# Attention over pooled pixels, then a gated MLP: the second batch's pixels loaded uncast, added in rows by GpSimd and pooled in pairs, and 17 GELU chunks on VectorE

## The chip, the cores and the metric

The kernel runs on one core of one Trainium2 chip. The metric is the device time of one launch in microseconds; a kernel's time is the median over its runs. A profile is one execution with the hardware profiler on; its span goes from the first to the last instruction of the program.

## The reference

Four batches of 12,288 queries attend to keys made from 384 x 32 pixels of 128 channels. Pixels are averaged over 4 x 4 windows, which leaves 768 rows per batch, and one product with `w_sr` gives both keys and values. The result goes through a two-layer MLP with a sigmoid-gated GELU.

```
kv_pool = kv.reshape(B, H // 4, 4, W // 4, 4, C).mean(axis=(2, 4))
k = v = kv_pool.reshape(B, -1, C) @ w_sr            # 768 x 128 for each batch
a = softmax((q @ k.transpose(0, 2, 1)) / sqrt(C))
x = (a @ v).reshape(B * 12288, C)
h = x @ w_in                                        # d_ff = 2048
out = (h * (1 / (1 + exp(-1.702 * h)))) @ w_out
```

## The kernel before

The 49,152 queries are cut into 96 groups of 512 (`NG`), 24 to a batch. A batch's 768 keys are six chunks of 128 (`JC`), the 2,048 hidden units 16 chunks (`FCH`). The work has four stages: attention for groups 0 to 47, the MLP for them, attention for groups 48 to 95, the MLP for them. In the trace they begin at about 9, 145, 490 and 607 us.

A step is a pair of a TensorE part and one ScalarE instruction. `fill_attn` (L340, L342) makes the scores of up to three chunks in a set of three PSUM banks, and ScalarE takes their exponential into one of 102 slots of `ag`; `fill_moe` (L586, L588) does the same for the MLP with GELU. The drains use the slots up: `drain_attn` multiplies the exponentials with the values (L353, 129 columns, the last one giving the sum), and VectorE divides (L376, L379) into the resident tile `x`; `drain_moe` (L596) multiplies with `w_out`, VectorE transposes the result (L607) and SP's queue stores it. `x` holds 24,576 query rows. It is stored to HBM and loaded back transposed in parts (`put_away` L493, `bring_back` L499, both on SP's queue), since the MLP wants it with channels on partitions.

The order of every queue is written at build time by one loop at the end of the function. It keeps a running time `now`, counted in steps of about one 512-column matmul, predicts when ScalarE and VectorE finish (`end`, `dve`, with the costs `FIXED`, `CHUNK`, `COST`, `COPY`, `RECIPROCAL`), and places fills two steps ahead of ScalarE with drains and small extras between them. At run time each engine takes its instructions in that order and waits on semaphores. Four PSUM banks serve as accumulators for the drains and extras; after the narrow opening steps two of them remain.

Some chunks never go to ScalarE. `rolling` score chunks and the scores of groups 48 to 51 (`early`) are computed by TensorE in `early_fill` (L405) and exponentiated by VectorE with a polynomial (`early_exp`). `lent` chunks of the last stage are GELUs computed by VectorE (`lent_gelu`, L443 to L465, after the matmul L399); they go into `aside`, a ring of three chunks. A drain of a group with a lent chunk is placed only when the plan says that the chunk is made.

`background(i)` and `background_moe(g)` run when the first step of a group is placed. They put DMAs on the queues: `cast_q` (L209, GpSimd's queue) casts 2,048 queries from float32 to bfloat16 in HBM, at the groups in `CAST`; `load_qT` (L215, SP's queue) loads them transposed into one of four `qT` buffers, at the groups in `TURN`. `gate()` writes one number on VectorE and overwrites it on GpSimd, so that GpSimd's queue doesn't run ahead of VectorE's place in the order. The weights of the MLP are loaded at groups 27 and 28 (L541, L544).

Keys come about in two ways. Batches 2 and 3 are summed by accumulating DMAs (`add_kv`, L173) during the MLP stages. Batches 0 and 1 are pooled by TensorE: `load_chunk` (L130, GpSimd's queue) loads 128 half pixel rows, cast to bfloat16, into a part of `x` that is not yet used; `pool_chunk` (L139) multiplies them with the 0/1 matrix `sum4`, 16 matmuls of 32 columns that sum four pixel rows and four pixels of a row; VectorE copies the result (L142), and `key_and_value` (L161 to L164) makes the chunk of keys and of values. For batch 1 the six loads are put on the queue at groups 10 and 12, the pools become extras at groups 15 to 20 and the keys one group later each; group 24 is the first that needs them.

```
if i in (10, 12):
    gate()
    for jc in range(i % 10 * 3 // 2, i % 10 * 3 // 2 + 3):
        load_chunk(1, jc)
```

Of the kernel before, what the change touches and what calls it, by code (L numbers as in the profile page):

```python
# [7 lines left out]
F32 = mybir.dt.float32  # L8
F32R = mybir.dt.float32r
I32 = mybir.dt.int32  # L10
BF = mybir.dt.bfloat16
AF = mybir.ActivationFunctionType
AX = mybir.AxisListType
ADD = mybir.AluOpType.add
# [10 lines left out]
def kernel(  # L25
    ctx, tc, q, kv, w_sr, moe_w_in, moe_w_out, out,
):
    nc = tc.nc
    B, N, C = q.shape
    _, H, W, _ = kv.shape  # L30
    r = 4
    Hp, Wp = H // r, W // r
    J = Hp * Wp
    JC = J // 128
    d_ff = moe_w_in.shape[1]
    FCH = d_ff // 128
    scale = 1.0 / (C ** 0.5)
    G = 512
    SG = 4 * G
    NG = B * N // G  # L40
    NS = NG // 4
    GB = NG // B
# [10 lines left out]
    kv_r = kv.rearrange("b (ch p) (a w) c -> b a ch p (w c)", p=128, a=2)  # L53
# [6 lines left out]
    XS = NS // R  # L60
# [7 lines left out]
    kvtmp = ctx.enter_context(tc.tile_pool(name="kvtmp", bufs=1))  # L68
# [3 lines left out]
    opool = ctx.enter_context(tc.tile_pool(name="op", bufs=3))  # L72
# [12 lines left out]
    def acc(key=None):  # L85

        nonlocal last_acc
        last_acc = next_acc()
        turns.append(last_acc)
        turns.remove(last_acc)  # L90
        if key:
            closes[last_acc] = key
        return banks[:, last_acc, :]

    def next_acc():
        return min((m for m in turns if m not in closes), key=lambda m: (max(free[m], now), turns.index(m)))
# [12 lines left out]
    x = xpool.tile([128, XS * SG], BF, name="x")  # L109

    def x_tile(s):
        return x[:, s % XS * SG:(s % XS + 1) * SG]
# [3 lines left out]
    HC = H // 128  # L116
    h = J // 2
    kv_tiles, kv_sums, pooled, pTs, kTs, vs = {}, {}, {}, {}, {}, {}

    def new_keys(b):  # L120
        kTs[b] = kvres.tile([128, J], BF, name="kT")

        vs[b] = kvres.tile([128, JC, C + 8], BF, name="v")
        nc.vector.memset(vs[b][:, :, C:C + 1], 1.0)

    def load_chunk(b, jc):

        a, ch = divmod(jc, HC)
        t = x_tile(XS - 1 - jc)
        nc.gpsimd.dma_start(out=t, in_=kv_r[b, a, ch])  # L130
        kv_tiles[b, jc] = t.rearrange("p (wp w1 c) -> p w1 wp c", w1=r, c=C)

    def pool_chunk(b, jc):
# [7 lines left out]
        pTs[b, jc] = kvtmp.tile([128, 128], BF, name="pTc", bufs=2)  # L141
        nc.vector.tensor_copy(pTs[b, jc], ps[:, 0:128])  # L142

    def key_chunk(b, jc):
        if jc == 0:
            new_keys(b)
        ps = acc()
        nc.tensor.matmul(ps[:, 0:128], w_sr_sb, pTs[b, jc], start=True, stop=True)
        nc.vector.tensor_copy(kTs[b][:, jc * 128:jc * 128 + 128], ps[:, 0:128])
# [5 lines left out]
        vs[b, jc] = True  # L155

    def key_and_value(b, jc):
        if (b, jc) == (1, 0):
            new_keys(b)
        ps = acc()  # L160
        nc.tensor.matmul(ps[:, 0:128], w_sr_sb, pTs[b, jc], start=True, stop=True)  # L161
        nc.tensor.matmul(ps[:, 128:256], pTs.pop((b, jc)), w_sr_sb, start=True, stop=True)
        nc.vector.tensor_copy(kTs[b][:, jc * 128:jc * 128 + 128], ps[:, 0:128])  # L163
        nc.vector.tensor_copy(vs[b][:, jc, 0:C], ps[:, 128:256])  # L164
        vs[b, jc] = True
# [41 lines left out]
    def cast_q(s):  # L207
        sl = slice(s * SG, (s + 1) * SG)
        nc.gpsimd.dma_start(out=q_bf[sl, :].rearrange("(p i) c -> p (i c)", p=128),  # L209
                            in_=q_flat[sl, :].rearrange("(p i) c -> p (i c)", p=128))  # L210

    def load_qT(s):
        qTs[s] = qpool.tile([128, 1, SG], BF, name="qT")
        nc.vector.memset(qTs[s][:, 0, 0:1], 0.0)
        nc.sync.dma_start_transpose(out=qTs[s], in_=q_bf[s * SG:(s + 1) * SG, :])  # L215
# [53 lines left out]
    for m in range(0, 128, 32):  # L269
        p = slice(m, m + 32)  # L270
# [3 lines left out]
    sum4 = cpool.tile([128, 32], BF)  # L274
# [3 lines left out]
    w_sr_sb = cpool.tile([128, C], BF)  # L278
# [40 lines left out]

    early = range(NG // R, NG // R + EARLY)  # L320
    rolling = [(i, JC - 1) for i in [*range(38, NG // R, 6), *range(57, 90, 6)]]
    lent = [(g, FCH - 1) for g in range(52, 94, 3)]
    aside = agpool.tile([128, K, 512], BF, name="aside")

    def weights(c):
# [112 lines left out]
    def lent_gelu(ps, out):  # L438
# [23 lines left out]
        for m in (0, 256):  # L462
            nc.vector.reciprocal(b[:, m:m + 256], a[:, m:m + 256])  # L463
            yield RECIPROCAL
        nc.vector.scalar_tensor_tensor(out, raw, -LN2 / 1.702, b, MUL, MUL)  # L465
# [21 lines left out]
    PART, FIRST = 24, 3  # L487

    def put_away(n, m):
        size = PART // 2 if n == 0 and m > FIRST else PART  # L490
        for o in range(m * PART, m * PART + PART, size):
            lo = n * XS * SG + o * T
            nc.sync.dma_start(out=x_bf[lo:lo + size * T, :].rearrange("(k p) c -> p k c", p=T),  # L493
                              in_=x[:, o * T:(o + size) * T].rearrange("p (k c) -> p k c", k=size))

    def bring_back(n, m):
        o = m * PART
        lo = n * XS * SG + o * T
        nc.sync.dma_start_transpose(out=x[:, o * T:(o + PART) * T].unsqueeze(1), in_=x_bf[lo:lo + PART * T, :])  # L499
# [6 lines left out]
    def gate():  # L506

        one = gate_tile[:, gates[0] % 8:gates[0] % 8 + 1]
        gates[0] += 1
        nc.vector.memset(one, 0.0)  # L510
        nc.gpsimd.memset(one, 0.0)  # L511

    TURN = {6: 3, 7: 4, 8: 5, 20: 6, 21: 7, 22: 8, 30: 9, 32: 10, 35: 11, 40: 12}
    CAST = {0: [5], 13: [6], 14: [7], 15: [8], 25: [9, 10], 26: [11, 12]}
    CAST_MOE = {20: 13, 21: 14, 22: 15, 23: 16, 33: 17, 34: 18, 35: 19, 36: 20, 37: 21, 38: 22, 39: 23}

    def background(i):

        first_round = i < GB * 2
        s = TURN.get(i, NS) if first_round else i // 4 + 3 if i % 4 == 0 else NS  # L520
        if s < NS:
            load_qT(s)
        if i in CAST:
            gate()
            for s in CAST[i]:
                cast_q(s)
        if i in (10, 12):
            gate()
            for jc in range(i % 10 * 3 // 2, i % 10 * 3 // 2 + 3):
                load_chunk(1, jc)  # L530
        if 0 <= i - 16 < JC:
            extras.append((key_and_value, 1, i - 16))
        if 0 <= i - 15 < JC:
            extras.append((pool_chunk, 1, i - 15))
        if i in (28, 33, 38):
            put_away(0, (i - 28) // 5)
        if i in (31, 36, 41):
            bring_back(0, (i - 31) // 5)
        if i == 27:
            gate()  # L540
            nc.gpsimd.dma_start(out=w_in_sb, in_=moe_w_in)  # L541
        if i == 28:
            gate()
            nc.gpsimd.dma_start(out=w_out_sb, in_=moe_w_out.rearrange("(o p) c -> p o c", p=128))  # L544

# [33 lines left out]
    extras = []  # L579
# [67 lines left out]
    for n in range(R):  # L647
        part = [c for c in chunks if c[0] // (NG // R) == n]
        while part:
            m = sizes.pop(0) if sizes else K  # L650
# [12 lines left out]
        while flat:  # L663
            m = K if len(flat) > sum(rest) else rest.pop(0)
# [25 lines left out]
    def jobs(p):  # L690

        nonlocal now
        for f, *args in first.get(p, ()):
            if f in COST:
                now = max(now, free[next_acc()])
            f(*args)
            if f in COST:
                now += COST[f][0]
                free[last_acc] = copied(f)

    def prepare(p):

        nonlocal now
        kind, part = seq[p]
        for i, jc in part:
            if (kind, i) not in begun:
                begun.add((kind, i))
                (background if kind == "a" else background_moe)(i)
            while kind == "a" and ((key_and_value, i // GB, jc) in extras or (transpose_q, i) in extras):
                f, *args = extras.pop(0)  # L710
                now = max(now, free[next_acc()]) + COST[f][0]
                f(*args)
                free[last_acc] = copied(f)
# [20 lines left out]


    FIXED, CHUNK, SWITCH, HANDOVER, EVACUATE = 0.295, 1.978, 6.0, 1.0, 4.5
    COST = {pool_chunk: (1.9, 2.6), key_chunk: (0.3, 2.4), value_chunk: (0.3, 2.4),
            transpose_q: (1.05, 4.2), early_fill: (1.0, 5.5), key_and_value: (0.55, 3.5),
            transpose_pooled: (0.9, 3.6), make_k: (0.8, 3.2), make_v: (0.8, 3.7)}
    COPY = {pool_chunk: 1.5, key_chunk: 1.5, value_chunk: 1.5, key_and_value: 2.8, transpose_q: 3.2}  # L740
    SMALL = 0.26
    RECIPROCAL = 10.5
    PAUSE = 4.0
    end, extra_at = [], 0.0
    source, dve = None, 0.0
# [2 lines left out]
    def on_dve(cost):  # L748
        nonlocal dve
        dve = max(dve, now + 1.0) + cost  # L750


    def copied(f):
        if f not in COPY:
            return now + COST[f][1]
        on_dve(COPY[f])
        return max(now + COST[f][1], dve)

# [28 lines left out]
    for n in range(len(seq)):  # L787
        fill(n + 2)
        jobs(n + 3)
        while True:  # L790
# [33 lines left out]
            kind, i, c = source[0]  # L824
# [11 lines left out]
            start = now if source is todo_early else max(now, end[needs] + HANDOVER)  # L836
            if first_of:
                start = max(start, bank)
# [44 lines left out]
```

The softmax here doesn't subtract the row's maximum and nothing guards it: scores larger than these inputs give would overflow.

## Time and profile before

| | |
|---|---|
| time, median of 8 runs | 950.9 us (950.64 to 952.19) |
| profiled execution, its own time | 952.19 us |
| span of that execution | 950.4 us |
| ScalarE instructions, GELU over three chunks (L588) | 1,508 ns each as recorded, 510 with the narrower ones |
| TensorE matmuls of 512 columns (L586) | 379 ns each as recorded, x1522 |
| VectorE GELU, reciprocal of 256 columns (L463) | 1,726 ns, x28 |
| q loads, transposing (L215) | 4.4 us from issue to landing (median of 21) |
| pixel loads of batch 0 and 1 (L130) | 9.3 us from issue to landing (median of 12) |

The recorded lengths of matmuls and ScalarE instructions overlap, since the engines work in a pipeline; how often they start says more than how long one is. An engine's row of busy time counts neither its DMA issues nor its waits on semaphores. The first 13 us are the opening: loads of pixels and queries, the first pools and keys. After the last ScalarE instruction, at about 945 us, the last products, copies and stores follow.

### The profile page before, as it was taken

What the parts mean: (1) busy time and instruction counts of PE and PEld (TensorE: products, weight loads), DVE (VectorE), ACT (ScalarE), POOL (GpSimd) and SP (SyncE); (2) the same over time, 40 slices, a digit from 0 to 9 for tenths busy, and PEclk for the clock granted to TensorE, in tenths of its full rate; (3) what the DMA queues carried; (4) which work ended last, traced back from release to release, by engine and by line L of the source; (5) the groups of instructions that cost most, each with busy time, mean ns of one, the idle gap of its engine ahead of it and who ended that gap; (6) DMA issues with size and microseconds to landing.
All of it is one profiled execution on the core that took longest, in us unless ns stands there. A gap on an engine that the chain in (4) does not pass through costs nothing.

```text
span 950.4 us, 15424 instructions
## 1 busy us (share of the span) xinstructions
PE 940.6 (99%) x6314; PEld 502.8 (53%) x6314; DVE 536.6 (56%) x1037; ACT 933.9 (98%) x708; POOL 67.1 (7%) x115
## 2 busy tenths in 40 slices
PE   7999999999999999999999999999999999999998
PEld 4677677444444444444446777754444444444444
DVE  5643553102477777778655775465666665556631
ACT  5999999999999999999999999999999999999998
POOL 4101001330000242000000000000000000000000
DMA  9999931999876899764435683662222222222222
GB/s 181 208 176 188 206 69 35 156 125 171 166 136 100 125 149 126 116 107 78 67 56 105 133 163 80 134 122 34 44 34 45 34 46 34 45 33 45 34 45 45
DMA packets 372871, 94.93 MB, mean 100 GB/s; under 512 B 346736, under 2 KB 370416, under 8 KB 372464
## 3 DMA queue, kind: packets, MB, share of 16 engines
q1 hardware_dynamic: 343872, 61.31, 36.8%
q0 software_dynamic: 28656, 32.51, 22.6%
q8 instruction: 49, 0.80, 0.4%
q14 instruction: 22, 0.18, 0.1%
q10 hardware_dynamic: 272, 0.13, 0.0%
HBM read 52.49 MB, written 48.76 MB: 107 GB/s over the span
## 4 chain that ended last, share of the span: by engine, by line
ACT 88%; PE 9%; DMA 2%; issue 0%; DVE 0%; POOL 0%; POOLq 0%
ACT ag L588 71%; ACT ag L342 17%; PE banks L340 4%; PE banks L353 3%; DMA qT<-q_bf 1%; DMA x<-in_kv_dram 1%; PE banks L139 0%; PE banks L586 0%; PE banks L624 0%; ACT L588 0%; PE banks L596 0%; PE banks L233 0%; ACT L342 0%; DVE kT L163 0%; POOL x L222 0%
## 5 line engine op out<-in xcount | busy, mean ns | idle before, releaser
L588 ACT ACTIVATE ag<-banks 128x1536 bf16<-128x1536 f32 (+1 forms) x510 | 682.2, 1508 | 0.0
L586 PE MATMUL banks<-x,w_in_sb 128*128 128x512 bf16 x1522 | 411.7, 379 | 0.1
L596 PE MATMUL banks<-ag,w_out_sb 128*128 128x512 bf16 x1506 | 407.8, 379 | 0.0
L342 ACT ACTIVATE ag<-banks 128x1536 bf16<-128x1536 f32 (+2 forms) x192 | 245.8, 1442 | 5.0 <-PE banks L340 4.7
L596 PEld LDWEIGHTS <-w_out_sb 128*128 128x128 bf16 x1520 | 148.4, 98 | 178.1 <-issue 0.9
L586 PEld LDWEIGHTS <-w_in_sb 128*128 128x128 bf16 x1522 | 147.3, 98 | 170.4 <-issue 1.1
L607 DVE STREAM_TRANSPOSE o_sb<-banks 128x512 f32<-128x512 f32 x95 | 67.9, 715 | 210.9 <-PE banks L596 201.7
L353 PEld LDWEIGHTS <-ag 128*128 128x128 bf16 x2272 | 146.1, 98 | 46.4 <-issue 0.6
L353 PE MATMUL banks<-v,ag 128*128 128x129 bf16 x2272 | 163.7, 220 | 0.1
L340 PE MATMUL banks<-qT,kT 128*128 128x512 bf16 x544 | 148.7, 379 | 1.6 <-DVE kT L163 1.0
L432 DVE SCALAR_TENSOR_TENSOR ea<-ea,eb 128x512 f32<-128x512 f32 x128 | 87.9, 687 | 3.2
L376 DVE RECIPROCAL rec<-banks 128x3 f32<-128x3 f32 x124 | 22.2, 179 | 96.0 <-PE banks L353 96.0
L379 DVE TENSOR_TENSOR x<-banks,rec 128x384 bf16<-128x384 f32 x124 | 69.1, 558 | 4.3
L340 PEld LDWEIGHTS <-kT 128*128 128x128 bf16 x544 | 46.3, 98 | 26.6 <-DVE kT L163 1.7
L463 DVE RECIPROCAL eb<-ea 128x256 f32<-128x256 f32 x28 | 47.6, 1726 | 0.5
L173 POOL DMA_DIRECT2D kvs<-in_kv_dram x32 | 40.5, 1311 | 17.2 <-DMA kvs<-in_kv_dram 13.7
L421 DVE TENSOR_SCALAR ea<-banks 128x512 f32<-128x512 f32 x32 | 22.1, 691 | 34.0 <-PE banks L405 33.7
L456 DVE SCALAR_TENSOR_TENSOR ea<-ea,eb 128x512 f32<-128x512 f32 x56 | 38.3, 685 | 1.6
L511 POOL MEMSET gate_tile<- 1x1 f32 x37 | 3.9, 105 | 327.9 <-DVE gate_tile L510 327.9
L427 DVE SCALAR_TENSOR_TENSOR eb<-eb,ea 128x512 f32<-128x512 f32 x32 | 22.1, 690 | 0.9
L443 DVE TENSOR_SCALAR qT<-banks 128x512 f32<-128x512 f32 x14 | 9.7, 691 | 17.2 <-PE banks L399 16.9
L434 DVE SCALAR_TENSOR_TENSOR ag<-ea,ee 128x512 bf16<-128x512 f32 x24 | 16.5, 688 | 0.7
(84 smaller groups left out, 266.1 us busy)
## 6 DMA issues: line engine op xcount, KB each, us to landing
out_dram<-o_sb SPq DMA_DIRECT2D x380, 64.0 KB, 2.0
kvs<-in_kv_dram POOLq DMA_DIRECT2D x32, 384.0 KB, 6.4
q_bf<-in_q_dram POOLq DMA_DIRECT2D x21, 512.0 KB, 6.7
x_bf<-x SPq DMA_DIRECT2D x12, 768.0 KB, 5.7
x<-in_kv_dram POOLq DMA_DIRECT2D x12, 512.0 KB, 9.3
x_bf<-x SPq DMA_DIRECT2D x8, 384.0 KB, 4.6
x<-in_q_dram POOLq DMA_DIRECT2D x5, 256.0 KB, 15.1
w_in_sb<-in_moe_w_in_dram POOLq DMA_DIRECT2D x1, 512.0 KB, 11.6
```

The costliest lines, as they stand in the source:

```text
L173: nc.gpsimd.dma_start(out=kv_sums[b][:, i2], in_=kv_p[b, i, w, :, i2], **({"accum_op": ADD} if n else {}))
L340: nc.tensor.matmul(ps[:, k, :], kTs[i // GB][:, jc * 128:(jc + 1) * 128], rhs, start=True, stop=True)
L342: nc.scalar.activation(place([("a",) + c for c in chunks]), ps, AF.Exp, scale=scale)
L353: nc.tensor.matmul(av_of[u][:, k * (C + 1):(k + 1) * (C + 1)], weights(("a", i, jc))[:, o:o + T], vs[i // GB][:, jc, 0:C + 1], start=(jc = ...
L379: nc.vector.tensor_tensor(to, ps[:, :, 0:C], rec.unsqueeze(2).broadcast_to([128, TS, C]), MUL)
L432: nc.vector.scalar_tensor_tensor(a, a, COEFFS[k], b, ADD, MUL)
L456: nc.vector.scalar_tensor_tensor(a, a, COEFFS[k], b, ADD, MUL)
L463: nc.vector.reciprocal(b[:, m:m + 256], a[:, m:m + 256])
L586: nc.tensor.matmul(ps[:, k, :], w_in_sb[:, fc * 128:(fc + 1) * 128], x[:, g % (4 * XS) * G:(g % (4 * XS) + 1) * G], start=True, stop=True)
L588: nc.scalar.activation(place([("m",) + c for c in chunks]), ps, AF.Gelu_apprx_sigmoid)
L596: nc.tensor.matmul(o_of[g], w_out_sb[:, fc, :], weights(("m", g, fc)), start=(fc == 0), stop=(fc == FCH - 1))
L607: nc.vector.transpose(o_sb, o_of.pop(g))
```

## The change

Batch 1's pixels are loaded in float32, without a cast, from SP's queue (`load_pixels`), three chunks at group 10 and one each at groups 11, 12 and 13, into three places in `x` of twice the size; chunks 3 to 5 reuse the places of chunks 0 to 2. GpSimd adds the four pixels of a row for each pooled column with three tensor additions per chunk (`sum_pixels`, groups 11 to 16), the last of them into bfloat16, in a buffer of the output pool. TensorE then sums over the four pixel rows alone, two chunks at a time (`pool_sums`, 8 matmuls of 32 columns, extras at groups 16, 19 and 22), and `key_pair` makes two chunks of keys and values at groups 17, 20 and 23. The planner gets costs for the two.

The lent GELU chunks of the last stage are those of 17 groups instead of 14, and the planner's cost of a VectorE reciprocal is lower. The cast of q tile 9 goes from group 25 to 16, its load from group 30 to 24; tiles 10 to 12 are cast in two and one instead of with tile 9; the weights of the MLP are loaded one group earlier each. Parts 2 and 3 of the first stage's `x` are stored in halves, as the later ones were.

```diff
--- before.py
+++ after.py
@@ -141,6 +141,51 @@
         pTs[b, jc] = kvtmp.tile([128, 128], BF, name="pTc", bufs=2)
         nc.vector.tensor_copy(pTs[b, jc], ps[:, 0:128])
 
+    held, sums = {}, {}
+
+    def load_pixels(jc):
+
+        a, ch = divmod(jc, HC)
+        o = (XS - JC) * SG + jc % 3 * 2 * SG
+        t = x[:, o:o + 2 * SG].bitcast(F32)
+        if jc < 3:
+            nc.vector.memset(t[:, 0:1], 0.0)
+        nc.sync.dma_start(out=t, in_=kv_r[1, a, ch])
+        kv_tiles[1, jc] = t.rearrange("p (wp w1 c) -> p w1 wp c", w1=r, c=C)
+
+    def sum_pixels(jc):
+
+        t = kv_tiles.pop((1, jc))
+        if jc % 2 == 0:
+            held[jc // 2] = opool.tile([128, 512], F32, name="o_sb").bitcast(BF)
+        sums[jc] = held[jc // 2][:, jc % 2 * 512:jc % 2 * 512 + 512].rearrange("p (wp c) -> p wp c", c=C)
+        nc.gpsimd.tensor_tensor(t[:, 0], t[:, 0], t[:, 1], ADD)
+        nc.gpsimd.tensor_tensor(t[:, 2], t[:, 2], t[:, 3], ADD)
+        nc.gpsimd.tensor_tensor(sums[jc], t[:, 0], t[:, 2], ADD)
+
+    def pool_sums(b, jc):
+
+        ps = acc()
+        for k in range(2):
+            for wp in range(4):
+                o = k * 128 + 32 * wp
+                nc.tensor.matmul(ps[:, o:o + 32], sums[jc + k][:, wp, :], sum4, start=True, stop=True)
+        pTs[b, jc] = kvtmp.tile([128, 256], BF, name="pTp")
+        nc.vector.tensor_copy(pTs[b, jc], ps[:, 0:256])
+
+    def key_pair(b, jc):
+        if jc == 0:
+            new_keys(b)
+        ps = acc()
+        pT = pTs.pop((b, jc))
+        nc.tensor.matmul(ps[:, 0:256], w_sr_sb, pT, start=True, stop=True)
+        for k in range(2):
+            nc.tensor.matmul(ps[:, 256 + k * 128:384 + k * 128], pT[:, k * 128:(k + 1) * 128], w_sr_sb,
+                             start=True, stop=True)
+        nc.vector.tensor_copy(kTs[b][:, jc * 128:(jc + 2) * 128], ps[:, 0:256])
+        nc.vector.tensor_copy(vs[b][:, jc:jc + 2, 0:C], ps[:, 256:512].rearrange("p (k c) -> p k c", k=2))
+        vs[b, jc] = vs[b, jc + 1] = True
+
     def key_chunk(b, jc):
         if jc == 0:
             new_keys(b)
@@ -155,8 +200,6 @@
         vs[b, jc] = True
 
     def key_and_value(b, jc):
-        if (b, jc) == (1, 0):
-            new_keys(b)
         ps = acc()
         nc.tensor.matmul(ps[:, 0:128], w_sr_sb, pTs[b, jc], start=True, stop=True)
         nc.tensor.matmul(ps[:, 128:256], pTs.pop((b, jc)), w_sr_sb, start=True, stop=True)
@@ -319,7 +362,7 @@
 
     early = range(NG // R, NG // R + EARLY)
     rolling = [(i, JC - 1) for i in [*range(38, NG // R, 6), *range(57, 90, 6)]]
-    lent = [(g, FCH - 1) for g in range(52, 94, 3)]
+    lent = [(g, FCH - 1) for g in range(52, 94) if g % 5 in (2, 4)]
     aside = agpool.tile([128, K, 512], BF, name="aside")
 
     def weights(c):
@@ -487,7 +530,7 @@
     PART, FIRST = 24, 3
 
     def put_away(n, m):
-        size = PART // 2 if n == 0 and m > FIRST else PART
+        size = PART // 2 if n == 0 and m > 1 else PART
         for o in range(m * PART, m * PART + PART, size):
             lo = n * XS * SG + o * T
             nc.sync.dma_start(out=x_bf[lo:lo + size * T, :].rearrange("(k p) c -> p k c", p=T),
@@ -510,8 +553,8 @@
         nc.vector.memset(one, 0.0)
         nc.gpsimd.memset(one, 0.0)
 
-    TURN = {6: 3, 7: 4, 8: 5, 20: 6, 21: 7, 22: 8, 30: 9, 32: 10, 35: 11, 40: 12}
-    CAST = {0: [5], 13: [6], 14: [7], 15: [8], 25: [9, 10], 26: [11, 12]}
+    TURN = {6: 3, 7: 4, 8: 5, 20: 6, 21: 7, 22: 8, 24: 9, 32: 10, 35: 11, 40: 12}
+    CAST = {0: [5], 13: [6], 14: [7], 15: [8], 16: [9], 25: [10, 11], 26: [12]}
     CAST_MOE = {20: 13, 21: 14, 22: 15, 23: 16, 33: 17, 34: 18, 35: 19, 36: 20, 37: 21, 38: 22, 39: 23}
 
     def background(i):
@@ -524,22 +567,25 @@
             gate()
             for s in CAST[i]:
                 cast_q(s)
-        if i in (10, 12):
-            gate()
-            for jc in range(i % 10 * 3 // 2, i % 10 * 3 // 2 + 3):
-                load_chunk(1, jc)
-        if 0 <= i - 16 < JC:
-            extras.append((key_and_value, 1, i - 16))
-        if 0 <= i - 15 < JC:
-            extras.append((pool_chunk, 1, i - 15))
+        if 10 <= i < 10 + JC:
+            if i > 10:
+                sum_pixels(i - 11)
+            for jc in range(3) if i == 10 else [i - 8] if i < 14 and i > 10 else []:
+                load_pixels(jc)
+        if i == 10 + JC:
+            sum_pixels(JC - 1)
+        if i in (16, 19, 22):
+            extras.append((pool_sums, 1, (i - 16) // 3 * 2))
+        if i in (17, 20, 23):
+            extras.append((key_pair, 1, (i - 17) // 3 * 2))
         if i in (28, 33, 38):
             put_away(0, (i - 28) // 5)
         if i in (31, 36, 41):
             bring_back(0, (i - 31) // 5)
-        if i == 27:
+        if i == 26:
             gate()
             nc.gpsimd.dma_start(out=w_in_sb, in_=moe_w_in)
-        if i == 28:
+        if i == 27:
             gate()
             nc.gpsimd.dma_start(out=w_out_sb, in_=moe_w_out.rearrange("(o p) c -> p o c", p=128))
 
@@ -706,7 +752,7 @@
             if (kind, i) not in begun:
                 begun.add((kind, i))
                 (background if kind == "a" else background_moe)(i)
-            while kind == "a" and ((key_and_value, i // GB, jc) in extras or (transpose_q, i) in extras):
+            while kind == "a" and ((key_pair, i // GB, jc // 2 * 2) in extras or (transpose_q, i) in extras):
                 f, *args = extras.pop(0)
                 now = max(now, free[next_acc()]) + COST[f][0]
                 f(*args)
@@ -734,12 +780,12 @@
 
 
     FIXED, CHUNK, SWITCH, HANDOVER, EVACUATE = 0.295, 1.978, 6.0, 1.0, 4.5
-    COST = {pool_chunk: (1.9, 2.6), key_chunk: (0.3, 2.4), value_chunk: (0.3, 2.4),
+    COST = {pool_chunk: (1.9, 2.6), pool_sums: (1.1, 3.2), key_pair: (1.1, 5.0), key_chunk: (0.3, 2.4), value_chunk: (0.3, 2.4),
             transpose_q: (1.05, 4.2), early_fill: (1.0, 5.5), key_and_value: (0.55, 3.5),
             transpose_pooled: (0.9, 3.6), make_k: (0.8, 3.2), make_v: (0.8, 3.7)}
-    COPY = {pool_chunk: 1.5, key_chunk: 1.5, value_chunk: 1.5, key_and_value: 2.8, transpose_q: 3.2}
+    COPY = {pool_chunk: 1.5, pool_sums: 2.1, key_pair: 4.2, key_chunk: 1.5, value_chunk: 1.5, key_and_value: 2.8, transpose_q: 3.2}
     SMALL = 0.26
-    RECIPROCAL = 10.5
+    RECIPROCAL = 8.2
     PAUSE = 4.0
     end, extra_at = [], 0.0
     source, dve = None, 0.0
```

## The prediction

> **What bounds the kernel now.** I read the page first: busy shares, then the windows of the last stage, then the chain of waits and the list of waits for the few places where the busy engines stop.
>
> ```profile
> PE 940.6 (99%) x6314; PEld 502.8 (53%) x6314; DVE 536.6 (56%) x1037; ACT 933.9 (98%) x708; POOL 67.1 (7%) x115
> ```
>
> Two engines are full at once, TensorE and ScalarE. A busy TensorE row is modelled, so it must be counted. Windows of 50 us in the last stage, TensorE's first, ScalarE's second:
>
> ```profile
> 650.00:700.00 50.00, 50.00 (x233) 1.00 0.25 39
> 700.00:750.00 50.00, 50.00 (x233) 1.00 0.27 42
> ```
> ```profile
> 650.00:700.00 50.00, 50.00 (x38) 1.00 0.25 39
> 700.00:750.00 50.00, 50.00 (x39) 1.00 0.27 42
> ```
>
> 233 matmuls of 512 columns in 50 us, with one cut at each edge, are one per 0.2165 us, the pace of three in 0.65 us that the chain shows elsewhere. So TensorE's queue really has no hole, and neither has ScalarE's. What either saves comes out of the time only as far as the other saves as much. The chain in order of time (start, length, what):
>
> ```profile
> 41.31 0.65 PE banks L340 x3
> 41.95 0.85 PE banks L353 x15
> ...
> 56.38 0.65 PE banks L340 x3
> 57.03 0.39 PE banks L139 x16
> ...
> 93.21 8.70 DMA qT<-q_bf
> 101.90 0.05 issue
> 101.95 0.39 PE banks L405
> ...
> 103.19 5.33 ACT ag L342 x4
> ...
> 620.89 29.52 ACT ag L588 x22
> ```
>
> It gives all prices: 0.0565 us for a value matmul (15 in 0.85), 0.0245 us for a pooling one (16 in 0.39), 1.342 us for one ScalarE instruction over three chunks (22 in 29.52). It also shows the one large hole after the first 20 us: at 93.21 a transposing load of q is issued, lands 8.7 us later, and L405, an early score matmul for VectorE, waits for it. In the list of waits of 100 to 144 us (total, times, longest):
>
> ```profile
> ACT ag L342 <- PE banks L340: 1.4, 1, 1.4
> PEld L405 <- DMA qT<-q_bf: 1.5, 1, 1.5
> ```
>
> TensorE stands still from 100.4 to 101.9 and ScalarE with it for 1.4 us; both then run on without a hole, so it is lost to the end. Windows of 6 us, the last two columns being the share of the DMA engines and GB/s:
>
> ```profile
> 42.00:48.00 6.00, 2.19 (x6) 1.00 1.07 211
> 48.00:54.00 6.00, 1.23 (x5) 1.00 1.06 211
> 54.00:60.00 6.00, 0.00 (x0) 1.00 1.25 262
> 60.00:66.00 6.00, 0.00 (x0) 1.00 0.43 91
> ```
>
> Six pixel loads and three casts of q, each reading 1 MB, fill the DMA engines from about 41.5 (where three q transposes end) to about 63: 2.4 us each.
>
> **What the Trainium skill says.** "Perfetto Trace Analysis", Identifying the Most-Contended Engine: matmul busy time is no measure of how close TensorE is to its limit. Agreed: I count pitches. "TensorE: Matmul & The Clock Gate", Back-to-back issue gap: N/2.4 + 2.5 ns, and about 25 ns as a floor; the trace has 216.5 ns at 512 columns and 24.5 ns at 32, so a 32-column matmul is all floor, and fewer of them is the only saving. "DMA: Bandwidth & Descriptors", Issuing engines are not separate DMA queues: they share 16 engines. So moving the loads from GpSimd's queue to SP's gives no bandwidth; no run here shows it yet. "SBUF — State Buffer", SBUF: two separate sides: GpSimd and VectorE lock each other out where VectorE reads two SBUF inputs or uses a two-port mode. Between 41 and 70 us VectorE runs L376, L379 and copies, all with their large input from PSUM, so I count no conflict; the trace has no GpSimd add to test it.
>
> **The change part by part.**
>
> *TensorE, pooling.* Out: 6 x 16 pooling matmuls, 96 x 0.0245 = 2.35 us. In: 24, 0.59 us. The key and value matmuls keep their columns (12 of 128 against 3 of 256 and 6 of 128): 0.67 us either way. Saved: 1.76 us.
>
> *ScalarE, 17 lent chunks in place of 14.* Three chunks fewer make 245 instead of 246 three-chunk instructions in the last stage: 1.34 us. TensorE computes the lent scores anyway, so nothing there.
>
> *VectorE for it.* One lent chunk from the group rows is 0.69 + 3 x 0.43 + 0.69 + 0.42 + 4 x 0.69 + 0.69 + 0.42 + 2 x 1.73 + 0.66 = 11.1 us; three more are 33 us, on an engine that is 56% busy. What matters is lateness. In the trace a lent chunk takes 12.6 to 15.2 us from first to last instruction and is then used 11.7 to 19.3 us later. Counting matmuls in the changed program's order, the use stands 24.3 us or more behind its score matmul, and starts are at least 15.1 us apart. 15.2 of 24.3 leaves 9 us. Cost: nothing; if the cover were gone, TensorE would wait.
>
> *The q load of tile 9*, with its cast, moves from group 30 to 24. A group lasts 2.68 us (two steps of 1.34), so 93.2 becomes about 77; with the same 8.7 us it lands by 86, and L405 wants it at 100.4. The 1.5 us hole goes: 1.4 us on ScalarE. Next late could be its cast, now behind the adds on GpSimd's queue: issued near 64.5, it has 12 us; casts took 6.0 to 13.3 us to land while three stood in line, so this is close but covered by 14 us more. On SP the first storing of x (74.97 before) now stands behind this load and starts by 82; its reload, held behind the q load until 98.2 before, follows from about 88. Neither is needed before the stage at 143.7. Weight loads one group earlier: nothing.
>
> *GpSimd's adds.* 18 additions of 512 elements. The trace has none. "GPSIMD Engine Reference", 3.1, has 4497 ns for 2048 elements; a quarter is 1.12 us, and I take 1.2 with dispatch (an estimate). Bounds: 0.77 us (its one-input rate at 512 elements) and 2.2 (twice the quarter, for strided rows and the type change). The first pixels land near 41.5 + 2.4 + 0.6 = 44.6, as SP issues them when its q transposes are out (39.5). Then 3.6 us a chunk, plus 0.55 for a gate and cast at the third to sixth: sums of chunks 1, 3 and 5 end at 51.8, 60.1 and 68.4. The loads of chunks 3 to 5 wait for the sum three before and land within some 4.5 us; each has two sums, 7 us, to do so. In the changed order the three pools stand 2.4, 10.3 and 18.2 us of matmuls behind the place where the first pool ran (53.1): 55.5, 63.4, 71.3. Spare: 3.7, 3.3, 2.9 us. So the adds cost nothing as long as one takes less than about 1.34 us (44.6 + 18t + 2.2 = 71.0). Behind a late add stand on GpSimd the casts of q 7 to 9, on SP the pixel loads and then q tiles 6 to 9; a pool that waits stops TensorE and ScalarE directly. VectorE sheds 18 copies of 0.29 us and gets 9 wider ones: not on the path.
>
> *Sum.* TensorE 1.76 + 1.5 = 3.3 us, ScalarE 1.34 + 1.4 = 2.75 us. The smaller decides; small waits of the old pools (0.1 to 0.2 us at three places on ScalarE) may give a little more, so 2.9. The profiled execution took 952.19 us (span 950.4, 1.8 around it), so 949.3 of its kind; it is the slowest of eight, 1.3 over the median. Against the median 950.9: **948.0 us**.
>
> **Rivals.**
>
> 1. *The hole moves instead of closing.* The early exponential at 100 us meets another wait, or the three lent chunks bring a like one. Then only work counts: 950.9 - 1.34 = 949.5. For it: no slack anywhere, so any new hole shows. Against: nothing else near 100 us waits in the list.
> 2. *GpSimd's first add loads its code.* The changed program has a library reload ahead of the first add; the same page, 2.1, prices a first call at about 6 us. Its place is after the cast at 18.5, with GpSimd idle until the gate at 38.7, so it should be hidden. If it strikes only with the first add, sums end 6 us later, at 57.8, 66.1, 74.4: TensorE is held 3.4 us in all (later lateness contains the earlier): 951.4.
> 3. *Slower: adds at 2 us or more.* GpSimd becomes the bound of the pools: chunk 5 ends at 44.6 + 36 + 2.2 = 82.8, 11.8 us after 71.0, giving 948.0 + 11.8 = 959.8. It decides from 1.34 us per add on, and loses the whole gain of 2.9 at 1.50 us. For it: 1.2 is no measurement of this chip. Against: it needs 1.8 times the page's figure.
> 4. *The lent chunks come late* (VectorE the bound): needs 9 us more per chunk than measured.
>
> **How the numbers follow.** Forecast 0.62 (own range 947.2 to 948.9); rival 1 0.14; rival 2 0.10; rival 3 0.11; rival 4 and the rest 0.03. A change under 0.2% (1.9 us) can't be told from none. Faster by more: the forecast, 0.62, and a little of rival 1: 0.63. Within: most of rival 1 and about two thirds of rival 2 and the mild end of rival 3: 0.22. Slower: 0.15. The range goes down to 947.0, for the old pools' small waits, and up to 951.8, taking in rivals 1 and 2; beyond it lies most of rival 3.
>
> **What would show it.** Adds: their mean length below 1.34 us, the last one's end before the third pool, no wait of the pool matmuls for GpSimd. The hole: no wait of the early score matmul for q near 100 us. Pools: 24 matmuls, about 0.2 us a pool of two. Lent chunks: 245 ScalarE instructions, no wait on the lent buffer. Wrong is the forecast if pools wait for GpSimd, or if TensorE shows a new hole over 1 us before 145 us.

## The result and the profile after

The changed kernel takes 958.71 us at the median of 12 runs, from 951.45 to 962.8; the kernel before took 950.91 beside it. The ratio is 1.0073, with a 95% interval of 1.0058 to 1.0088: slower by 0.6 to 0.9%. (A ratio takes in all runs, so it isn't the quotient of the two medians.) On the chip of the first experiments it took 953.85 us (951.35 to 963.28, ratio 1.0046, 1.0027 to 1.0065). Not only the middle moved: 32 runs of the kernel before lie within 2.4 us, 12 of the changed one are spread over 11.4. The profiled execution took 953.70 us and is one of the better ones.

Busy shares of the kernel after, from its page:

```profile
PE 942.2 (99%) x6239; PEld 502.4 (53%) x6239; DVE 567.9 (60%) x1075; ACT 932.8 (98%) x707; POOL 85.8 (9%) x126
```

Both full engines are as full as before, and the hole at 100 us is gone: no wait for q stands in the list of waits from 100 to 144 us. The new waits are earlier. From the list of waits of 66 to 144 us (total, times, longest):

```profile
...
ACT ag L385 <- PE banks L383: 3.9, 2, 3.6
DVE pTp L174 <- PE banks L172: 3.3, 1, 3.3
POOL x L162 <- DMA x<-in_kv_dram: 3.2, 1, 3.2
PEld L172 <- POOL o_sb L164: 2.6, 1, 2.6
PE banks L172 <- POOL o_sb L164: 2.5, 1, 2.5
```

Read from the line of L162 on: GpSimd's first addition of a chunk (L162) waits 3.2 us for pixels, the third pool (L172) waits 2.5 us for the last sum, ScalarE waits 3.6 us for scores. The chain of waits (start, length, what) shows it in order of time:

```profile
57.99 12.34 DMA x<-in_kv_dram
70.33 0.07 issue
70.41 1.26 POOL x L162
71.66 1.23 POOL x L163
72.89 0.07 issue
72.96 1.27 POOL o_sb L164
74.23 0.05 issue
74.28 0.29 PE banks L172 x4
74.57 0.97 PE banks L396 x9
75.54 1.28 PE banks L383 x3
76.82 1.06 PE banks L396 x12
77.88 0.65 PE banks L383 x3
```

The load of the last pixel chunk is issued at 57.99 and takes 12.34 us. Then the lines after 74.28: three score matmuls take 1.28 us where they take 0.65 at 77.88. TensorE's clock was halved. The windows of 6 us of the same profile have it in the first number after the engines, the granted clock (the share of its full clock that TensorE was given):

```profile
66.00:72.00 6.00, 5.77 (x65) 4.12 (x63) 2.59 (x10) 6.00 (x6) 2.76 (x5) 1.00 1.14 168
72.00:78.00 6.00, 3.72 (x30) 2.77 (x31) 1.16 (x3) 2.38 (x2) 2.14 (x2) 0.72 0.85 86
...
74.07:77.49 3.42, 3.21 (x25) 2.38 (x26) 1.16 (x3) 0.63 (x1) 0.15 (x1) 0.50 1.01 94
```

The last line is the window cut to the stretch itself: 3.42 us at 0.50. "TensorE: Matmul & The Clock Gate" of the Trainium skill, What's actually happening, tells of such a state: after an idle window of about 3.4 us the array's clock is halved until it has been busy for one. The trace has the half clock and the length of 3.4 us; but here a hole of 2.66 us between two matmuls was enough. (A hole is counted here from one start of a matmul to the next, less their usual pace: 71.59 to 74.28.)

Its length isn't all that counts. In this trace the clock goes down at 74.07, up at 77.49, and next down at 951.30, when the matmuls are over: the first two are 3.413 us apart, the last two 873.81, which is 256 times as much. In the other traces, too, the changes of one execution lie a multiple of 3.413 us apart. So in these traces the clock changes only at the lines of a fixed grid of such stretches, and the grid lies differently against the program in each execution. The stretch before the half clock (its length, the busy time and matmuls of TensorE, the granted clock):

```profile
70.66:74.07 3.41, 1.11 (x14) 1.00 0.62 60
```

The hole lay almost wholly inside it and left 1.11 us of work. A hole of nearly the same length that falls across a line does no such harm; the last experiment has one.

So the execution adds up. A version of the changed kernel without holes (the one with its casts kept apart, below) has a span of 947.4 us; 947.4 + 2.66 for the hole + 1.7 for 3.4 us at half speed gives 951.8, and the span is 951.9.

The additions themselves are nearly as long as was assumed, 1.27 us where the prediction had 1.2, by the groups of GpSimd's instructions (count, busy time, mean ns, idle before):

```profile
L162 POOL TENSOR_TENSOR x<-x 128x512 f32<-128x512 f32 x6 | 7.6, 1270 | 30.6 <-DMA x<-in_kv_dram 30.6
L164 POOL TENSOR_TENSOR o_sb<-x 128x512 bf16<-128x512 f32 x6 | 7.6, 1269 | 0.5
L163 POOL TENSOR_TENSOR x<-x 128x512 f32<-128x512 f32 x6 | 7.6, 1262 | 0.0
```

### The profile page after: what moved, and what is told of

The parts are those of the page before. It is cut to its first block, busy times and chain, and to the rows that moved or that the text cites. A ratio compares the mean times of both kernels' runs of the same rounds, so it can differ in the third digit from the quotient of the medians.

```text
span 951.9 us, 15345 instructions
## 1 busy us (share of the span) xinstructions
PE 942.2 (99%) x6239; PEld 502.4 (53%) x6239; DVE 567.9 (60%) x1075; ACT 932.8 (98%) x707; POOL 85.8 (9%) x126
## 4 chain that ended last, share of the span: by engine, by line
PE 94%; DMA 4%; POOL 2%; issue 0%; DVE 0%; SPq 0%; POOLq 0%
PE banks L642 35%; PE banks L632 35%; PE banks L396 12%; PE banks L383 11%; DMA x<-in_kv_dram 4%; PE banks L448 1%; POOL o_sb L164 1%; POOL x L162 1%; POOL x L163 1%; PE banks L442 0%; PE banks L670 0%; PE banks L276 0%; PE banks L139 0%; PE banks L227 0%; PE banks L242 0%
## 5 line engine op out<-in xcount | busy, mean ns | idle before, releaser
L383 PE MATMUL banks<-qT,kT 128*128 128x512 bf16 x544 | 149.4, 380 | 1.6 <-DVE kT L206 1.0
L475 DVE SCALAR_TENSOR_TENSOR ea<-ea,eb 128x512 f32<-128x512 f32 x128 | 87.7, 685 | 3.4 <-issue 0.2
L383 PEld LDWEIGHTS <-kT 128*128 128x128 bf16 x544 | 46.5, 98 | 26.2 <-DVE kT L206 1.7
L506 DVE RECIPROCAL eb<-ea 128x256 f32<-128x256 f32 x34 | 57.6, 1722 | 0.5
L499 DVE SCALAR_TENSOR_TENSOR ea<-ea,eb 128x512 f32<-128x512 f32 x68 | 46.6, 685 | 2.0
L486 DVE TENSOR_SCALAR qT<-banks 128x512 f32<-128x512 f32 x17 | 11.8, 691 | 22.5 <-PE banks L442 22.2
## 6 DMA issues: line engine op xcount, KB each, us to landing
x<-in_kv_dram POOLq DMA_DIRECT2D x6, 512.0 KB, 11.4
```

The lines of the kernel that those rows point to most:

```text
L383: nc.tensor.matmul(ps[:, k, :], kTs[i // GB][:, jc * 128:(jc + 1) * 128], rhs, start=True, stop=True)
L475: nc.vector.scalar_tensor_tensor(a, a, COEFFS[k], b, ADD, MUL)
L499: nc.vector.scalar_tensor_tensor(a, a, COEFFS[k], b, ADD, MUL)
```

## The experiments

The theory after this profile: the casts of q stand on GpSimd's queue behind the additions and reach the DMA engines later, there they hold up first the last pixel load and then the transposing loads of q; TensorE gets holes, and after a hole it may run at half clock. Rivals: the additions are too slow; VectorE's greater load makes the chip throttle.

**The changed kernel again**, twice, without an edit.

> The changed kernel once more, to see whether the wait moves from run to run. Theory (casts hold up the last pixel load, TensorE then idles before the third pool and runs at half clock for a while): another profile shows the same wait of the third pool for GpSimd near 72 us, of another length (1 to 8 us), and a granted clock under 1.0 right after it; runs spread over 951 to 963 us. Rival (the additions themselves are too slow): the wait has the same length as in the first profile within 0.3 us. Rival (the busier VectorE makes the chip throttle): low clock in the last stage, after 600 us, where VectorE is busiest.

> The changed kernel once more, one look, for the spread of its holes. Theory: the third pool waits 2 to 5 us for GpSimd's last sum; where that or the following wait for a q tile is over about 2.5 us, a stretch of half clock of 3.4 us or a multiple of it follows; span equals about 947.5 plus the holes plus half of the half-clock time.

Measured: the first profile has a hole of 2.2 us at the third pool and a span of 949.6, in a time of 951.35, and no half clock, so that part of its forecast failed. The second has 3.9 us there and 957.83 us. Its chain:

```profile
57.80 13.52 DMA x<-in_kv_dram
71.32 0.07 issue
71.39 1.26 POOL x L162
```

and its windows:

```profile
72.00:78.00 6.00, 2.73 (x20) 1.90 (x21) 1.16 (x3) 1.15 (x2) 3.13 (x3) 0.67 0.48 40
78.00:84.00 6.00, 6.00 (x55) 4.27 (x53) 1.80 (x7) 4.80 (x4) 0.00 (x0) 0.76 1.22 143
```

The hole varies with the landing of that load while an addition stays at 1.26 us, and the low clock follows the hole: 0.67 and 0.76 of two windows are 3.4 us lost, two stretches of 3.4 us at half clock. The first of the two, with the shorter hole, has 1.00 throughout. While TensorE works, no low clock lies after 600 us, against the theory of a throttle by VectorE. The sum for the second is 947.4 + 3.9 + some 3 = 954.3 against a span of 956.1. The rest comes after all the work: its last store lands 3.9 us after its issue, where it takes 1.9 in the version without holes (L681).

**Third pool one group later.**

```diff
-        if i in (16, 19, 22):
+        if i in (16, 19, 23):
-        if i in (17, 20, 23):
+        if i in (17, 20, 24):
```

> The third pool and its keys one group later (23 and 24), nothing else. 2.7 us more for the sums. Theory of the late load: a hole of 2.6 us as in the first profile just closes, so time 948 to 950 in most runs, a few later where the load is later still. Rival (throttle by VectorE's load): no difference from the changed kernel, 951 to 963.

Measured: 951.69 us at the median of 22 runs, from 949.62 to 962.55; ten of them lie at 949.6 to 950.9, nine at 956 to 963, and the ratio to the kernel before is 1.0034 (1.0012 to 1.0057). The ten are below the median of the kernel before, 951.0, as they should be with the hole at the pool gone; but 948 to 950 was forecast for most, and only four are under 950. The nine slow ones, and no others, have a mean clock of 0.998 or less. So this pool isn't all: the profile (951.95 us) has TensorE waiting for q, not for GpSimd (`PE banks L383 <- DMA qT<-q_bf`, 1.3 us).

**14 lent chunks in the changed kernel.**

```diff
-    lent = [(g, FCH - 1) for g in range(52, 94) if g % 5 in (2, 4)]
+    lent = [(g, FCH - 1) for g in range(52, 94, 3)]
```

> The changed kernel with 14 lent GELU chunks as before. Theory of the late load: the hole and the spread stay, and time is about 1.3 us above the changed kernel of the same runs. Rival (throttle by VectorE's load): the clock is 1.0 and the spread goes.

Measured: 954.97 us (953.74 to 964.04), 1.1 us above the changed kernel beside it. Seven of its eight executions have a mean clock of 0.998 or less, as nine of the changed kernel's thirteen have, so VectorE's greater load isn't the cause. Its profile fell on the worst run, 964.04 us, and shows the second kind of hole. From its list of waits of 60 to 95 us, and its chain:

```profile
...
PE banks L172 <- POOL o_sb L164: 4.7, 1, 4.7
POOL x L162 <- DMA x<-in_kv_dram: 4.7, 1, 4.7
PE banks L383 <- DMA qT<-q_bf: 4.1, 1, 4.1
```
```profile
66.35 20.50 DMA qT<-q_bf
86.85 0.04 issue
86.90 0.58 PE banks L383
87.48 1.30 PE banks L396 x12
```

The load of q tile 6, 4.0 us in the kernel before, takes 20.5 us here; the casts of tiles 8 and 9, issued at 63.0 and 67.3, are in flight with it. Group 24's first scores wait 4.1 us for it, and the value matmuls after that run at half clock again (12 in 1.30 us where 0.68 is usual). This execution adds up as well: 947.8 for the version without holes and with 14 chunks (below), 4.85 and 4.24 for the holes and 4.4 for the work at half clock make 961.3, which is its span.

**Casts of tiles 7 to 9 behind the last sum.**

```diff
-    CAST = {0: [5], 13: [6], 14: [7], 15: [8], 16: [9], 25: [10, 11], 26: [12]}
+    CAST = {0: [5], 13: [6], 17: [7], 18: [8], 19: [9], 25: [10, 11], 26: [12]}
```

> Casts of q tiles 7, 8 and 9 are placed at groups 17, 18 and 19, behind the last sum, in place of 14, 15 and 16. Theory of the casts: the last pixel load lands within 6 us of its issue (12.3 in the changed kernel), the sums are done before the third pool, no hole, clock 1.0, time 947.5 to 949. Rival (additions too slow): the third pool still waits over 1 us, time above 951. Rival (throttle by VectorE's load): clock still under 1.0 and a spread of several us.

Measured: 957.45 us (953.0 to 960.54). The forecast of the time was wrong and that of the mechanism right by half. The load of the last pixel chunk takes 6.8 us in place of 12.3, and the last sum ends at 69.3, 2 us ahead of the third pool, with the same additions and without a wait for pixels. (Three casts of some 0.55 us on GpSimd's queue no longer stand between the sums either.) But tiles 7 and 8, cast later, are also loaded later. The load of tile 8, landed at 83.4 in the changed kernel before the casts of tiles 10 to 12 begin at 84.2, is now issued at 79.9, and those casts (79.8 to 82.1) and the two loads of weights (82.6 and 83.8) with it:

```profile
79.91 26.76 DMA qT<-q_bf
106.68 0.04 issue
106.72 0.58 PE banks L383
```

26.8 us for a load that takes 4.4 in the kernel before, and 8.7 us of waiting at group 32. The harm had only moved.

**Casts kept apart from the q loads.**

```diff
-    CAST = {0: [5], 13: [6], 14: [7], 15: [8], 16: [9], 25: [10, 11], 26: [12]}
+    CAST = {0: [5], 13: [6], 17: [7], 18: [8], 19: [9], 28: [10, 11], 29: [12]}
-        if i == 26:
+        if i == 29:
...
-        if i == 27:
+        if i == 30:
```

The two conditions are those of the weights' loads.

> The changed kernel with its casts kept apart from the q loads: tiles 7 to 9 at groups 17 to 19, 10 to 12 at groups 28 and 29, the weights at 29 and 30. Theory: the loads of tiles 7 and 8 take under 10 us, no wait over 1 us near groups 24 to 36, clock 1.0, time 947.5 to 950 in most runs. Rival (additions or paired pools): still 951 to 963.

Measured: 949.45 us (949.2 to 951.45, 16 runs), ratio to the kernel before 0.9984 (0.9976 to 0.9991). It has all additions, pairs and lent chunks of the changed kernel and differs from it in when eight DMAs are issued (six casts and two loads of weights); the pixels still come uncast and from SP's queue, so neither of these alone is the cause. None of its executions has a mean clock under 0.999. In its profile the last pixel load takes 6.4 us, the q loads from 60 us on take at most 7.8 us, and no window between 66 and 102 us has a clock under 1.00, the one with the former hole among them:

```profile
72.00:78.00 6.00, 5.89 (x64) 4.20 (x64) 2.98 (x10) 6.00 (x5) 0.00 (x0) 1.00 0.85 178
```

ScalarE is busy for all of its 6.00 us. This is the version that beats both.

**Its twin with 14 lent chunks** (the edit shown above, in this version).

> The version with its casts kept apart, with 14 lent chunks in place of 17. If ScalarE sets the end once TensorE's pools are shorter: 1.3 us slower than that version, 950.8. If TensorE sets it: the same within 0.3 us.

Measured: 949.76 us, ratio 0.9987 (0.998 to 0.9993; the kernel before took 951.07 beside it). The three chunks are worth 0.3 us here, not 1.3; in the medians that is within the intervals. The end of the trace shows why. The timeline of the last 6 us (start, length, engine, line, what, count) of this kernel:

```profile
943.71 0.95 PE L670 MATMUL banks<-w_out_sb,ag 128*128 128x128 bf16 x14 [0.46 <-ACT ag L634]
...
944.30 0.27 ACT L678 COPY o_sb<-banks 128x128 f32<-128x128 f32 x1 [0.64 <-PE banks L670]
```

and of the one with 17:

```profile
941.79 2.45 PE L670 MATMUL banks<-w_out_sb,ag 128*128 128x128 bf16 x41
...
943.67 0.91 DVE L678 COPY o_sb<-banks 128x128 f32<-128x128 f32 x3 [3.31 <-PE banks L670]
943.88 0.27 ACT L678 COPY o_sb<-banks 128x128 f32<-128x128 f32 x1 [1.68 <-DMA out_dram<-o_sb]
```

L678 is the last copy, and the number in brackets how long ScalarE stood idle before it. The view puts that wait down to a DMA, but VectorE's copy just before it waits for TensorE, and in the second profile of the changed kernel the same wait is put down to TensorE too:

```profile
950.48 0.27 ACT L678 COPY o_sb<-banks 128x128 f32<-128x128 f32 x1 [1.68 <-PE banks L670]
```

I read it as a wait for the matmuls in all of these versions. With 14, TensorE has caught up: its last matmuls wait for ScalarE's last GELU (0.46 us). With 17, ScalarE is done 944.30 - 0.64 - (943.88 - 1.68) = 1.46 us earlier, about the 1.34 forecast, but 41 matmuls are still to run in a row, and it waits for them: the copy moves by 0.42 only.

**The kernel before with single parts of the change.** Lent chunks and the planner's reciprocal alone:

> The kernel before with 17 lent GELU chunks and the planner's lower cost of a reciprocal, nothing else. Theory: one ScalarE instruction less, TensorE's own work unchanged, so 0 to 1.3 us faster, 949.6 to 950.9, clock 1.0. Rival (VectorE's load makes the chip throttle): slower, clock under 1.0 after 600 us.

Measured: 951.26 us, ratio 1.0003 (0.9995 to 1.0012): nothing. Its timeline has the reason at the end:

```profile
944.07 3.23 PE L624 MATMUL banks<-w_out_sb,ag 128*128 128x128 bf16 x55 [0.30 <-DVE o_sb L607]
...
946.89 0.27 ACT L632 COPY o_sb<-banks 128x128 f32<-128x128 f32 x1 [2.87 <-DMA out_dram<-o_sb]
```

In the kernel before that copy is

```profile
946.88 0.27 ACT L632 COPY o_sb<-banks 128x128 f32<-128x128 f32 x1 [1.32 <-DMA out_dram<-o_sb]
```

ScalarE is done earlier, and then waits 2.87 us in place of 1.32 for matmuls that TensorE hasn't got to. Then q tile 9 alone:

```diff
-    TURN = {6: 3, 7: 4, 8: 5, 20: 6, 21: 7, 22: 8, 30: 9, 32: 10, 35: 11, 40: 12}
-    CAST = {0: [5], 13: [6], 14: [7], 15: [8], 25: [9, 10], 26: [11, 12]}
+    TURN = {6: 3, 7: 4, 8: 5, 20: 6, 21: 7, 22: 8, 24: 9, 32: 10, 35: 11, 40: 12}
+    CAST = {0: [5], 13: [6], 14: [7], 15: [8], 16: [9], 25: [10, 11], 26: [12]}
```

> The kernel before with the cast of q tile 9 at group 16 and its load at group 24 (the casts of tiles 10 to 12 as in the changed kernel), nothing else. The step of the prediction: the 1.5 us hole at 100 us goes, 949.4 to 949.6. Theory of the casts: holds only while that cast is off the DMA engines when tile 6 is loaded; it lands near 68 and tile 6 is issued at 66, so a few runs may be late.

Measured: 950.51 us, ratio 0.9991 (0.9983 to 0.9999), where 949.4 to 949.6 was expected. The hole at 100 us is gone from its profile, but its worth is 951.16 - 950.51 = 0.65 us. The prediction had priced the hole from the one execution profiled before, the longest of its eight runs. That the hole is shorter at the median is likely, but no such execution was profiled. The end of the timeline here:

```profile
942.45 3.07 PE L624 MATMUL banks<-w_out_sb,ag 128*128 128x128 bf16 x52
...
945.10 0.27 ACT L632 COPY o_sb<-banks 128x128 f32<-128x128 f32 x1 [1.32 <-DMA out_dram<-o_sb]
```

TensorE comes last, with 52 matmuls in a row. Beside the two versions above this tells what each saving brings in a profile: without the old pools the last copy goes from 945.10 to 944.30, where ScalarE sets it; with three GELU chunks less besides, to 943.88, where TensorE sets it. TensorE's end thus comes 945.10 - 943.88 = 1.22 us earlier.

**A cast put among q loads in the kernel before**, where GpSimd adds nothing:

```diff
-    CAST = {0: [5], 13: [6], 14: [7], 15: [8], 25: [9, 10], 26: [11, 12]}
+    CAST = {0: [5], 13: [6], 14: [7], 15: [8], 20: [9, 10], 26: [11, 12]}
```

> The kernel before, with the casts of q tiles 9 and 10 at group 20 instead of 25, so that they are on the DMA engines while q tiles 6, 7 and 8 are loaded transposed; no addition on GpSimd, no other change. Theory (a cast in flight makes a transposing q load several times longer): the loads of tiles 6 and 7 take 8 us or more from issue to landing (4.0 and 6.0 before), TensorE waits near groups 24 to 28 in some runs and then shows a half clock, and the time spreads upwards by several us. Rival (GpSimd's additions or the paired pools themselves cost the time): as before, 950.4 to 952.7, clock 1.0.

Measured: 951.37 us, ratio 1.0001 (0.9993 to 1.0009). The loads of tiles 6 and 7 take 11.6 and 8.2 us where they took 4.0 and 6.0, as expected; but TensorE waits for q only 0.9 us at 76 us, and the hole at 100 us is gone, perhaps because tile 10's cast is out of the way. So the contention is there without any addition, and two casts alone don't bring a hole long enough for the half clock. The spread that I expected didn't come.

**The changed kernel with the casts, q loads and weights at their old groups** (the edit of tile 9 undone, weights at 27 and 28).

> The changed kernel with the casts, the q loads and the weights at the groups of the kernel before; the uncast pixels, the sums, the pairs and 17 lent chunks stay. It tells whether the cast of tile 9 brought to group 16 does the harm, or already the casts of tiles 6 to 8 queued behind the additions. If the additions' place in GpSimd's queue is enough: the last pixel load still takes over 10 us, the third pool waits 2 us or more, the time is above 951 with a spread. If the cast of tile 9 does it: 948.5 to 950.5, tight.

Measured: 956.28 us (953.74 to 957.61, 6 runs). Its waits from 60 to 110 us:

```profile
POOL x L162 <- DMA x<-in_kv_dram: 3.4, 1, 3.4
...
PE banks L448 <- DMA qT<-q_bf: 2.4, 1, 2.4
...
PE banks L172 <- POOL o_sb L164: 1.9, 1, 1.9
```

The additions' place ahead of the casts is enough to make the last pixel load late; moving tile 9 isn't needed for it. That hole and the old one at 100 us add up: 947.4 + 2.0 + 2.6, and 2 us for a late last store as in the second repetition of the changed kernel, make the span of 954.1. Clock 1.00 held through both. The hole at 101 us is 2.6 us long, hardly shorter than the one that halved the clock in the profile of the result. But a line of the grid of 3.413 us, at 102.50, cuts it in two:

```profile
99.08:102.50 3.42, 2.54 (x28) 1.00 1.84 177
102.50:105.91 3.41, 1.85 (x22) 1.00 0.93 200
```

Neither stretch is as empty as the one with 1.11 us of work. In the traces of this case, 1.85 us of work in a stretch kept the clock up and 1.11 didn't; where between them the edge lies is open.

## Why the prediction was wrong

*What bounds the kernel* was read rightly: both engines are full, and "what either saves comes out of the time only as far as the other saves as much". The lent chunks alone bring nothing; beside TensorE's saving they bring 0.3 us. What the reading lacked is which of the two comes last, and by how much: in the profile of the version with tile 9 moved, ScalarE's end is followed by 1.32 us of matmuls. So the first 0.8 us came from TensorE.

*The sum of the parts*, without the new holes: the version with its casts apart takes 949.45 us where 950.51 is taken with tile 9 alone, in the same comparison. These 1.06 us are to be set against the 1.34 of ScalarE, the smaller saving; the profiles have 1.22 for TensorE, of 1.76 forecast, and where its other 0.5 us went isn't traced. Against the kernel before it is 951.16 - 949.45 = 1.7 us in all, where 2.9 was forecast. Of the missing 1.2 us, 0.75 is the hole of tile 9 (1.4 forecast, 0.65 measured); the rest stays open, at the edge of what the intervals tell. The prediction's sum against the profiled execution's own time, 949.3, lies close to this version; taken over to the median it counted the profile's hole at its full length, where 0.65 us was to be had.

*The q load of tile 9*, 1.4 us: right in mechanism, mis-sized. It measured 0.65 us at the median. The warning stood in the prediction's own sum, which noted that the profiled run lay 1.3 us over the median, and didn't ask whether a longer hole than usual could be part of that.

*GpSimd's adds*: 1.2 us assumed, 1.27 measured, and no sign of a lock by VectorE or of a late code load. (The bound of 0.77 us is, in "GPSIMD Engine Reference" of the Trainium skill, 3.1, the best case of a tight loop over 512 elements; the page doesn't call it a one-input rate.) The sums of chunks 1 and 3 ended at 53.6 and 62.3, ahead of their pools. The step that failed, and turned a gain into a loss, is the next sentence: "The loads of chunks 3 to 5 wait for the sum three before and land within some 4.5 us; each has two sums, 7 us, to do so." They took 4.9, 7.6 and 12.3 us. I had each cast at 2.4 us of the DMA engines' time, counted that time as free, and forgot that the casts, issued between the sums, would be in flight with exactly the loads that the sums wait for. Sum 5 ended at 74.2 instead of 68.4. Of these 5.8 us, 3.2 are the wait for pixels. The other 2.6, from additions that began at 46.0 instead of 44.6 and were a little longer, had already used up most of the spare 2.9; alone they would still have been in time for the pool.

*"Next late could be its cast ... close but covered"*: named, but judged by landing times of casts in a row. What went wrong wasn't the cast's lateness, it was what a late cast does to the q load beside it: 9.3 to 20.5 us for tile 6 in the profiles of the changed kernel and of its version with 14 lent chunks, against 4.0. The kernel before issues its casts of tiles 6 to 8 at 47.6, 49.2 and 53.2, and all are landed at 65.8, before the first q load at 66.2. The change gave up this order by putting additions ahead of the casts on one queue.

*The price of a hole* was taken as its length. Where a hole left a stretch of the grid nearly empty, it cost up to 1.7 us besides, for each 3.4 us of half clock. The rivals had the place (a pool that waits for GpSimd) but a wrong cause (slow additions, from 1.34 us on), and the slower side got 0.15.

## What to carry to other kernels

An operation put on a queue delays every DMA issued behind it; look where those DMAs land now and which transfers they meet, not only whether they land in time. A cast, which in these traces holds a DMA engine for 2.4 us with one packet of 32 KB, and a transposing load, which comes in packets of 256 bytes, should be kept apart in time, even when the engines have room on average. Before pricing a hole from a single profile, compare that execution with the median: here a hole of 1.4 us in the profile was worth 0.65 us at the median.

## What the runs showed that was not expected

A transposing load of 512 KB of q took 4.0 us with no cast in flight, 8.2 and 11.6 us with two, and 20.5 and 26.8 us at worst. TensorE's clock halved for one, two or three stretches of 3.4 us after holes of 2.66, 3.9 and 8.8 us, and did not after 2.2 and 2.6 us; the 2.66 us lay almost wholly within one stretch of a fixed grid of 3.413 us, the 2.6 us across two. So a load that lands a few microseconds later in one run than in another became a spread of 11 us in the time.
